# Two turned tiles instead of eight, v in runs for four, half-array third blocks, single row sums: a linear-attention and token-mixer kernel on one Trainium2 core

## The chip, the cores and the metric

The kernel runs on one core of a Trainium2 chip. The core has a matrix engine (TensorE, PE in the profile; its weight loads are PEld), a vector engine (VectorE, DVE), a scalar engine (ScalarE, ACT), a general engine (GpSimd, POOL) and a queue engine (SyncE, SP) that here only issues transfers. Each engine works through its own list of instructions in order. Sixteen DMA engines carry the transfers that SP and POOL issue. SBUF is the on-chip memory, PSUM the eight accumulator banks of PE. The metric is the device time of one execution in microseconds (us); lower is better.

## What is computed

Inputs `r, k, v, w, a, b` have the shape 4 x 8 x 768 x 40 (batch, heads, time, width), in 32-bit floats. A recurrence over time gives 768 rows of 320 numbers (8 heads x 40) for each of the four batches, and a mixer with one matrix over tokens and two over channels follows:

```python
for t in range(S):
    y[:, :, t] = np.einsum('bhd,bhde->bhe', rt, state)
    Sa = np.einsum('bhde,bhe->bhd', state, at)
    state_decay = state * wt[:, :, None, :] - np.einsum('bhd,bhe->bhde', Sa, bt)
    state = state_decay + np.einsum('bhd,bhe->bhde', vt, kt)
...
theta = x @ w_theta                       # x: the y of all heads side by side
zr, zi = x * np.cos(theta), x * np.sin(theta)
yr = np.einsum('ts,bsd->btd', w_tok_r, zr)
yi = np.einsum('ts,bsd->btd', w_tok_i, zi)
u = x + yr + yi
return u + np.maximum(u @ w_ch, 0.0)
```

## The kernel before

**Tiles.** Time is cut into tiles of 128 steps: six for each batch, 24 in all, numbered 0 to 23. A tile passes through these steps; the names are those of the program's list.

- *Loads.* w of every tile comes by one load of 160 KB (`raw_w`, line 465), 1,024 pieces of 160 bytes. r comes for two tiles at once in "runs": eight steps in a row are one piece of 1,280 bytes, 320 KB in all (line 481). For tiles below `RUNS` (8), v comes in runs too, and for tiles below `TURNED` (8) also k, b and a. All other k, b, a and v come by single loads of 160 KB (line 465). Buffers: four for w and for k and b, six for a and v. SP issues all loads in list order and stands still where a buffer has not been read yet.
- *Decay.* ACT takes the logarithm of w (`ln`, line 509); PE sums it over the tile (`cs`, line 518); ACT exponentiates (`exp`, or `exp1` and `ew` from tile 8 on).
- *Features of an unturned tile.* POOL multiplies k and b (`kb`) and a (`ah`) by the decays (line 493) and casts v (line 499). PE turns 16 blocks, or twelve where v came in runs (`tt`, line 419), and ACT or DVE evicts them to `feat` (`et`, lines 452 and 456).
- *Features of a turned tile.* Casts put the runs of k, b and a of two tiles into the order for turning (line 499), PE turns them into PSUM (`tkbr`, `tar`), PE also forms the summed logarithms in turned form (`csT`, line 604), ACT exponentiates them (lines 611 and 613), and DVE multiplies the turned k, b and a out of PSUM (lines 625 and 628). k and b are then turned back (`tbk`). v in runs is cast, turned (`to`), evicted by ACT (line 642) and turned back (`tb`, line 653).
- *Scores.* Products of k and a, b and a, v and r, nu and r in eight matmuls on array halves each (line 668): `spsi`, `sphi`, `slv`, `slu`. DVE multiplies by a triangular mask while it evicts (line 676), or ACT evicts (line 678) and POOL clears the triangle (line 680).
- *Recurrence and output.* Small products (lines 707 to 745) give the correction nu and the new state; lines 821 to 834 give the tile's output x.

**The mixer.** For two tiles at a time, x is turned in blocks of 128 columns (`xt`). The 320 columns of a tile are two blocks and a half; the buffers `xp` and `up` have 64 further columns of zeros behind the two tiles, so that each tile's third block can be read 128 wide, and the third block of the weights `wth` and `wch` has zeros in its lower 64 rows. `mixed` (line 804) runs six matmuls of 320 columns for a pair, three for each tile. ACT takes sine and cosine (line 859), and POOL forms z (line 493). After a batch, `mix_row` (line 881) multiplies z by the token matrices: twelve matmuls of 320 columns for each tile, the two tiles of a pair into the two banks of one double bank, then one DVE addition for both (`uadd2`, line 891). u is turned (`ut`), `mixed` multiplies by `wch`, DVE adds (line 915), and SP stores (line 918). Tiles 22 and 23 go through the mixer one by one.

**Order.** Nothing is ordered by the chip. `Plan.add` numbers some 1,370 operations; `ORDER` is a written-out list of these numbers, and each engine gets its operations in that order. `HOMES` gives the PSUM banks in the order in which they are taken. `PICK` names the operations that run in their other form: another engine, or a turn of whole blocks (line 424) instead of array halves (line 419). `WARM` puts fill matmuls (line 983) in front of some operations. Row and column weights are loaded by POOL (lines 927 and 935).

**Modes.** An operation on PE uses the whole array or its two halves of 64 rows, two matmuls at a time; the list mixes both.

Of the kernel before, what the change touches and what calls it, by code (L numbers as in the profile page):

```python
# [10 lines left out]
BF16 = mybir.dt.bfloat16  # L11
# [7 lines left out]
RUNS = 8  # L19
TURNED = 8  # L20
LATE = 8
ORDER = [
# [225 lines left out]
def kernel(  # L248
# [14 lines left out]
    nc = tc.nc  # L263
# [26 lines left out]
    def load(i):  # L290
# [5 lines left out]
        if i < TURNED:  # L296
            return ([("raw_w", s), raw_w[s], src(w)],)
# [98 lines left out]
    for t in (wth, wch):  # L396
        nc.vector.memset(t[rows(1), 2], 0.0)
# [64 lines left out]
    def loads(i):  # L462
# [8 lines left out]
        if i < RUNS:  # L471
            sets.append((v, raw_o[i // 2 % 3], "o"))
# [559 lines left out]
```

## Time and profile before

| | us |
|---|---|
| three runs | 201.14, 203.02, 204.42 |
| median | 203.02 |
| profiled execution, its span (the page gives no other time of it) | 201.1 |

| | instructions | busy us |
|---|---|---|
| PE | 4,254 | 185.6 |
| DVE | 270 | 165.1 |
| ACT | 298 | 161.6 |
| POOL | 166 | 138.1 |

A row of the page's groups has the line, the engine, the operation, its output and inputs with their shapes, how often, then the busy time in us, the mean duration in ns, and the idle time of the engine just before with what ended it. A row of a timeline has the start, the time taken, the engine, the line and what was done. PE's matmuls overlap: a duration contains the way through the array, so what one matmul costs PE is read from start to start. A row of the windows table has a stretch of the span, the busy time of each engine in it, the clock that PE was granted, the busy share of the DMA engines and what they moved. Consecutive instructions on ACT and DVE overlap by about a tenth of a microsecond.

### The profile page before, as it was taken

The numbers are of one execution on the slowest core, as the hardware profiler recorded it, in microseconds if no ns is written. First come the engines' busy times: TensorE is split into PE (matmuls) and PEld (weight loads), VectorE is DVE, ScalarE is ACT, GpSimd is POOL, SyncE is SP. The second block draws the span as 40 slices with busy tenths as digits, with TensorE's granted clock in tenths as the row PEclk, the third lists the DMA queues.
The fourth block names the chain that finished last, engine by engine and source line by source line (L and its number), as shares of the span: only waits on it lengthen the run. The fifth ranks groups of instructions, "written<-read, shape, count | busy, mean of one in ns | idle before, by whom it ended". The sixth has DMA issues, their size and how long they took to land.

```text
span 201.1 us, 9549 instructions
## 1 busy us (share of the span) xinstructions
PE 185.6 (92%) x4254; PEld 148.0 (74%) x4254; DVE 165.1 (82%) x270; ACT 161.6 (80%) x298; POOL 138.1 (69%) x166
## 2 busy tenths in 40 slices
PE   7689898996799898999999999999999999999992
PEld 7467686875787776787786878877887877877761
DVE  7599899997899899898988898798796859872462
ACT  2699999987899899878999979798999859585000
POOL 6355346790498989889959973979988984659000
PEclk9999999999999999999999999999999999999999
DMA  5999978999839999989999799736894010000332
GB/s 150 268 324 312 255 186 182 241 167 201 143 56 196 184 162 191 175 180 176 193 162 205 161 169 262 138 68 133 152 211 139 0 68 3 3 3 0 134 113 83
DMA packets 104888, 30.90 MB, mean 154 GB/s; under 512 B 92432, under 2 KB 104848, under 8 KB 104848
## 3 DMA queue, kind: packets, MB, share of 16 engines
q1 hardware_dynamic: 102416, 27.53, 62.2%
q0 software_dynamic: 2432, 2.77, 8.2%
q8 instruction: 33, 0.54, 1.1%
q14 instruction: 7, 0.06, 0.1%
HBM read 29.13 MB, written 3.93 MB: 164 GB/s over the span
## 4 chain that ended last, share of the span: by engine, by line
PE 61%; ACT 17%; DVE 14%; issue 2%; DMA 2%; SPq 1%; ACTq 0%
PE ps L881 19%; PE ps L668 8%; PE ps L804 8%; PE ps L419 8%; PE ps L424 4%; DVE lam L676 3%; PE ps L827 3%; DVE psi L676 3%; DMA raw_w<-in_w_dram 2%; ACT feat L452 2%; PE ps L712 2%; PE ps L745 2%; PE ps L724 2%; ACT exw L613 2%; PE ps L707 2%
## 5 line engine op out<-in xcount | busy, mean ns | idle before, releaser
L676 DVE TENSOR_TENSOR lam<-ps,mask_p 128x1024 bf16<-128x1024 f32 x37 | 44.9, 1219 | 4.9 <-PE ps L668 4.7
L881 PE MATMUL ps<-z,wtok 128*128 128x320 bf16 x288 | 47.5, 299 | 0.0
L493 POOL TENSOR_TENSOR z<-cs,xp 128x640 bf16<-128x640 f32 x21 | 29.8, 1430 | 2.8 <-ACT cs L859 2.8
L881 PEld LDWEIGHTS <-wtok 128*128 128x128 bf16 x288 | 24.9, 97 | 9.0
L493 POOL TENSOR_TENSOR kb<-raw_kb,ex 128x640 bf16<-128x640 f32 x16 | 22.9, 1431 | 4.3 <-DMA raw_kb<-in_b_dram 2.1
L668 PEld LDWEIGHTS <-feat 64*128 64x128 bf16 x576 | 18.3, 94 | 7.9 <-issue 5.3
L676 DVE TENSOR_TENSOR psi<-ps,mask_p 128x1024 bf16<-128x1024 f32 x18 | 21.8, 1216 | 0.3 <-PE ps L668 0.2
L676 DVE TENSOR_TENSOR phi<-ps,mask_n 128x1024 bf16<-128x1024 f32 x16 | 19.5, 1220 | 2.2 <-PE ps L668 2.1
L668 PE MATMUL ps<-feat 64*128 64x128 bf16 x384 | 18.6, 217 | 2.3 <-DVE phi L676 0.7
L827 PE MATMUL ps<-kb,lam 128*128 128x40 bf16 x384 | 15.6, 180 | 0.8 <-issue 0.8
L680 POOL TENSOR_SCALAR_AFFINE_SELECT lam<-lam 128x1024 bf16<-128x1024 bf16 x11 | 12.0, 1093 | 4.3 <-ACT lam L678 4.3
L827 PEld LDWEIGHTS <-lam 128*128 128x128 bf16 x384 | 13.8, 96 | 1.2 <-issue 0.9
L452 ACT COPY feat<-ps 128x1024 f32<-128x1024 f32 x14 | 14.2, 1020 | 0.7 <-PE ps L419 0.6
L728 ACT ACTIVATE nu<-ps 128x320 bf16<-128x320 f32 x24 | 10.8, 450 | 4.7 <-PE ps L724 4.5
L680 POOL TENSOR_SCALAR_AFFINE_SELECT phi<-phi 128x1024 bf16<-128x1024 bf16 x8 | 8.8, 1100 | 8.3 <-ACT phi L678 8.3
L642 ACT COPY rT<-ps 128x512 bf16<-128x512 bf16 x24 | 13.5, 602 | 1.2 <-PE ps L419 1.2
L493 POOL TENSOR_TENSOR ah<-raw_a,ex 128x320 bf16<-128x320 f32 x16 | 12.9, 807 | 2.2 <-ACT ex L540 2.1
L452 ACT COPY uT<-ps 128x384 f32<-128x384 f32 (+1 forms) x10 | 4.6, 463 | 11.8 <-PE ps L424 5.9
L915 DVE SCALAR_TENSOR_TENSOR oo<-ps,up 128x640 f32<-128x640 f32 x11 | 9.0, 822 | 6.0 <-PE ps L804 6.0
L509 ACT ACTIVATE lw<-raw_w 128x320 bf16<-128x320 f32 x24 | 11.7, 493 | 2.2 <-DMA raw_w<-in_w_dram 1.2
L625 DVE TENSOR_TENSOR feat<-ps,exi 128x512 bf16<-128x512 bf16 x16 | 10.4, 683 | 2.7 <-ACT exi L611 2.3
L718 ACT CAST nx<-ps 128x320 bf16<-128x320 f32 x24 | 10.5, 438 | 2.4 <-PE ps L712 2.1
(156 smaller groups left out, 557.1 us busy)
## 6 DMA issues: line engine op xcount, KB each, us to landing
raw_w<-in_w_dram SPq DMA_DIRECT2D x24, 160.0 KB, 4.6
raw_r<-in_r_dram SPq DMA_DIRECT2D x12, 320.0 KB, 4.8
out_dram<-oo SPq DMA_DIRECT2D x11, 320.0 KB, 3.1
raw_v<-in_v_dram SPq DMA_DIRECT2D x16, 160.0 KB, 4.6
raw_kb<-in_k_dram SPq DMA_DIRECT2D x16, 160.0 KB, 4.3
raw_kb<-in_b_dram SPq DMA_DIRECT2D x16, 160.0 KB, 4.4
raw_a<-in_a_dram SPq DMA_DIRECT2D x16, 160.0 KB, 4.4
raw_kb<-in_b_dram SPq DMA_DIRECT2D x4, 320.0 KB, 4.9
```

The costliest lines, as they stand in the source:

```text
L419: nc.tensor.transpose(out=dst[:, c, n * 64:n * 64 + 64], in_=block[rows(c)], identity=ident[rows(c), rows(c)])
L452: nc.scalar.copy(out=to, in_=source)
L493: pool = ("POOL", lambda: nc.gpsimd.tensor_tensor(out=dst, in0=in0, in1=in1, op=ALU.mult))
L509: add("ACT", "ln", i, lambda: nc.scalar.activation(out=heads(lw)[:, :, 0:D], in_=raw_w[s4], func=AF.Ln), 473, [("raw_w", s4)], [("lw", s2) ...
L642: add("ACT", "e" + nm, i + x, lambda x=x, dst=dst: nc.scalar.copy(out=dst.rearrange("p g (t q) -> p g t q", q=8), in_=ps(pr).bitcast(BF16) ...
L668: nc.tensor.matmul(t[:, q, g, :], lhsT=lhs[rows(q), g, :], rhs=rhs[rows(q), g, :], start=True, stop=True)
L676: add("DVE", kindm, i, lambda: nc.vector.tensor_tensor(out=flat, in0=whole(), in1=mask.to_broadcast([128, 2 * G, 128]), op=ALU.mult), 1217 ...
L680: add(None, "sel", i, None, 0, dkeys, dkeys, alts=(("POOL", lambda: nc.gpsimd.affine_select(out=flat, in_=flat, pattern=[[0, 2 * G], [1, 1 ...
L728: add("ACT", "enu", i, lambda: nc.scalar.mul(out=nu[:, :, 0:D], in_=ps(pk)[:, 0:DM].rearrange("p (h d) -> p h d", h=H), mul=-1.0), 437, [p ...
L804: nc.tensor.matmul(out, lhsT=lhs[:, 3 * c + kt, :], rhs=wt[:, kt, :], start=kt == 0, stop=kt == 2)
L827: nc.tensor.matmul(t[:, h * D:h * D + D], lhsT=lam[:, n, p, g, :], rhs=kb[:, n, h, 0:D], start=first and n == 0, stop=n == 1, skip_group_c ...
L881: nc.tensor.matmul(to, lhsT=wtok[t % NCH][:, c, s, :], rhs=z[:, c, s], start=s == 0 and c == 0, stop=s == NT - 1 and c == 1)
```

## The change

Six things change.

- `TURNED` goes from "below 8" to tiles 0 and 1, `RUNS` from "below 8" to tiles 0 to 3. Tiles 2 to 7 load k, b and a singly and form them on POOL; tiles 4 to 7 load v singly too.
- The zero columns of `xp` and `up` go. The 640 columns of two tiles are turned as five blocks; the middle one holds the last 64 columns of the first tile and the first 64 of the second. For the second tile `wth` and `wch` hold the rows a second time, shifted by 64, so there are four loads for each instead of two.
- For a pair `mixed` becomes two operations: four matmuls over whole blocks, and two over half blocks, one on each array half, into the two banks.
- A row sum takes one bank, and each tile has its own addition (`uadd`).
- `ORDER`, `HOMES` and `PICK` are new as a whole. Among other things the loads of w for tiles 1 and 0 now stand first in SP's list.
- `WARM` has two entries (44 fill matmuls) instead of nine.

The diff without the lists, whose old and new lines are left out:

```diff
-RUNS = 8
-TURNED = 8
+RUNS = frozenset(range(4))
+TURNED = frozenset(range(2))
...
-WARM = {19: (38, 0), 20: (2, 3), 21: (3, 2), 30: (6, 3), 44: (2, 3), 58: (4, 3), 106: (1, 2), 264: (2, 4), 274: (1, 4)}
+WARM = {21: (38, 0), 20: (6, 1)}
...
-        if i < TURNED:
+        if i in TURNED:
             return ([("raw_w", s), raw_w[s], src(w)],)
...
-                () if i < RUNS else ([("raw_v", i % 6), raw_v[i % 6], src(v)],))
+                () if i in RUNS else ([("raw_v", i % 6), raw_v[i % 6], src(v)],))
...
-    xp_t = padded("xp", [128, 2 * DM + 64], NX // 2, lambda t: t[:, 2 * DM:])
-    up_t = padded("up", [128, 2 * DM + 64], 2, lambda t: t[:, 2 * DM:])
-    xT_t = sb("xT", [128, 6, 128], BF16, NXT)
-    uT_t = sb("uT", [128, 6, 128], BF16, 2)
+    xp_t = sb("xp", [128, 2 * DM], BF16, NX // 2)
+    up_t = sb("up", [128, 2 * DM], BF16, 2)
+    xT_t = sb("xT", [128, 5, 128], BF16, NXT)
+    uT_t = sb("uT", [128, 5, 128], BF16, 2)
...
-    wth = consts.tile([128, 3, DM], BF16, name="wth")
-    wch = consts.tile([128, 3, DM], BF16, name="wch")
-    for t in (wth, wch):
-        nc.vector.memset(t[rows(1), 2], 0.0)
+    wth = consts.tile([128, 5, DM], BF16, name="wth")
+    wch = consts.tile([128, 5, DM], BF16, name="wch")
...
     def blocks_of(t):
-        return [t[:, c * DM + m:c * DM + m + 128] for c in range(t.shape[1] // DM)
-                for m in (0, 128, 256)]
+        return [t[:, m:m + 128] for m in range(0, t.shape[1], 128)]
...
+        def whole():
+            for c in range(2):
+                for kt in range(2):
+                    nc.tensor.matmul(ps(pk)[:, c, 0:DM], lhsT=lhs[:, 3 * c + kt, :],
+                                     rhs=wt[:, 3 * c + kt, :], start=kt == 0, stop=False,
+                                     skip_group_check=True)
+
+        def third():
+            for c in range(2):
+                nc.tensor.matmul(ps(pk)[:, c, 0:DM], lhsT=lhs[rows(c), 2, :],
+                                 rhs=wt[rows(c), 2, :], start=False, stop=True,
+                                 skip_group_check=True)
+        add("PE", kind, q, whole, 4 * mm(320), [lkey] + wkeys, [pk], at=at, new=(pk, 2),
+            tail=tail(320))
+        add("PE", kind + "3", q, third, mm(320), [lkey] + wkeys, [pk], at=at, mode=64,
+            tail=tail(320))
...
         for t in group:
+            pk = ("ps", "row", t)
             for s in range(NT):
-                def chunk(t=t, s=s):
-                    to = ps(pk)[:, 0:DM] if alone(q) else ps(pk)[:, t - q, 0:DM]
+                def chunk(t=t, s=s, pk=pk):
                     for c in range(2):
-                        nc.tensor.matmul(to, lhsT=wtok[t % NCH][:, c, s, :], rhs=z[:, c, s],
-                                         start=s == 0 and c == 0, stop=s == NT - 1 and c == 1)
+                        nc.tensor.matmul(ps(pk)[:, 0:DM], lhsT=wtok[t % NCH][:, c, s, :],
+                                         rhs=z[:, c, s], start=s == 0 and c == 0,
+                                         stop=s == NT - 1 and c == 1)
...
+            add("DVE", "uadd", t, lambda t=t, pk=pk: nc.vector.tensor_tensor(
+                out=u_of(t), in0=ps(pk)[:, 0:DM], in1=x_of(t), op=ALU.add), 488,
+                [pk, x_key(t)], [u_key(t)], at="row")
...
             pieces = ((dst[:, 0:2, :], src[0:256, :].rearrange("(a p) d -> p a d", p=128)),
-                      (dst[rows(0), 2, :], src[256:320, :]))
+                      (dst[rows(0), 2, :], src[256:320, :]),
+                      (dst[:, 3:5, :], src[64:320, :].rearrange("(a p) d -> p a d", p=128)),
+                      (dst[rows(1), 2, :], src[0:64, :]))
```

More of the change, by code (lines that the diff above doesn't have):

```diff
@@ L547, in prep @@
         fast = i < 2
-        if i >= TURNED:
+        if i not in TURNED:
             product("kb", i, kb[:, :, :, 0:D], raw_kb[s4],
@@ L798, in mixed, with go @@
         pk = ("ps", kind, q)
-        def go():
-            for c in range(1 if alone(q) else 2):
-                out = ps(pk)[:, 0:DM] if alone(q) else ps(pk)[:, c, 0:DM]
+        if alone(q):
+            def go():
                 for kt in range(3):
-                    nc.tensor.matmul(out, lhsT=lhs[:, 3 * c + kt, :], rhs=wt[:, kt, :],
+                    nc.tensor.matmul(ps(pk)[:, 0:DM], lhsT=lhs[:, kt, :], rhs=wt[:, kt, :],
                                      start=kt == 0, stop=kt == 2)
-        add("PE", kind, q, go, (3 if alone(q) else 6) * mm(320), [lkey] + wkeys, [pk], at=at,
-            new=(pk, 1 if alone(q) else 2), tail=tail(320))
+            add("PE", kind, q, go, 3 * mm(320), [lkey] + wkeys, [pk], at=at, new=(pk, 1),
+                tail=tail(320))
+            return
+        def whole():
[12 more added lines that the diff above has]
+        add("PE", kind + "3", q, third, mm(320), [lkey] + wkeys, [pk], at=at, mode=64,
+            tail=tail(320))
     def readout(i):
@@ L851, in sines @@
         cs, pk = cs_t[n % NCS], ("ps", "th", q)
-        mixed("th", q, xT_t[n % NXT], wth, [("wth", c) for c in range(2)], ("xT", n % NXT))
+        mixed("th", q, xT_t[n % NXT], wth, [("wth", c) for c in range(4)], ("xT", n % NXT))
         wide_ = 1 if alone(q) else 2
@@ L904, in channels @@
                uT_t[n][:, 0:len(blocks)], [("uT", n)], at="row")
-        mixed("ch", q, uT_t[n], wch, [("wch", c) for c in range(2)], ("uT", n), at="row")
+        mixed("ch", q, uT_t[n], wch, [("wch", c) for c in range(4)], ("uT", n), at="row")
         ck, oo = ("ps", "ch", q), oo_t[n]
@@ L928, in mixer_weights @@
                     out=to, in_=part), 580, [], [(key, c)], at="rel",
-                    work=260 if c else 1030)
+                    work=260 if c % 2 else 1030)
     def wtok_block(tb):
```

31 lines of the change are left out of this document (10 added, 21 removed), and 199 rows, old and new, of tables (HOMES, ORDER, PICK).

## The prediction

> **What bounds the kernel now.** I read the page first (busy shares, slices, queues), then the table by windows, then the chain of waits in order of time, and last the timelines of single engines around the places where the limit changes.
>
> ```profile
> PE 185.6 (92%) x4254; PEld 148.0 (74%) x4254; DVE 165.1 (82%) x270; ACT 161.6 (80%) x298; POOL 138.1 (69%) x166
> ...
> DMA  5999978999839999989999799736894010000332
> ...
> q1 hardware_dynamic: 102416, 27.53, 62.2%
> q0 software_dynamic: 2432, 2.77, 8.2%
> ```
>
> No engine is alone at the limit, and the DMA row is at 9 for most of the first 26 slices (5.03 us each). The windows separate the stages:
>
> ```profile
> core 0: us, PE busy (x) PEld busy (x) DVE busy (x) ACT busy (x) POOL busy (x), PEclk, DMA share, GB/s
> 0.00:80.60 80.60, 69.71 (x1798) 57.72 (x1799) 72.77 (x147) 71.27 (x135) 52.33 (x76) 1.00 0.92 201
> 10.00:20.00 10.00, 8.77 (x225) 7.14 (x223) 9.76 (x13) 9.93 (x22) 5.42 (x8) 1.00 1.09 318
> 50.00:60.00 10.00, 8.60 (x254) 7.46 (x249) 9.07 (x13) 9.31 (x18) 6.95 (x9) 1.00 0.57 101
> 80.00:85.00 5.00, 5.00 (x90) 3.70 (x89) 4.03 (x6) 4.50 (x10) 4.64 (x5) 1.00 0.98 171
> 87.70:201.10 113.40, 108.81 (x2294) 84.74 (x2288) 86.32 (x117) 84.05 (x152) 80.01 (x84) 1.00 0.55 118
> ...
> 190.00:201.00 11.00, 6.96 (x66) 4.59 (x63) 5.36 (x9) 0.80 (x2) 0.00 (x0) 0.97 0.29 100
> ```
>
> Up to 80.6 us DVE (72.77) and ACT (71.27) are nearly full and PE has 1,798 of its 4,254 matmuls behind it. From 87.7 us PE is busy for 108.81 of 113.40 us and the others have 27 us or more to spare. The chain shows the handover from DVE to PE:
>
> ```profile
> 75.39 1.13 DVE psi L676
> 76.53 1.79 DVE z L492
> 78.31 1.15 DVE phi L676
> 79.50 0.40 PE ps L668 x8
> 79.90 0.38 PE ps L881 x2
> ```
>
> So there is a first stage of about 80 us that DVE and ACT set, and a second that PE sets. The third resource, transfers, is hidden in the first stage, but not by much. Tile 12 marks the handover, and its last load and first product are these:
>
> ```profile
> 74.09 1.19 SPq L465 DMA_DIRECT2D raw_kb<-in_k_dram  x1
> ...
> 82.01 1.43 POOL L493 TENSOR_TENSOR kb<-raw_kb,ex 128x640 bf16<-128x640 f32 x1
> ...
> raw_kb<-in_k_dram SPq DMA_DIRECT2D x16, 160.0 KB, 4.3
> ```
>
> With the median of 4.3 us to landing, the load issued at 74.09 is there at 78.4; the product starts at 82.01. Only 3.6 us lie between, so the first stage can shrink by little before the transfers set it.
>
> **Fewer turned tiles: the engines.** Tiles 2 to 7 (six tiles) lose the decays in turned form and the products from PSUM:
>
> ```profile
> L625 DVE TENSOR_TENSOR feat<-ps,exi 128x512 bf16<-128x512 bf16 x16 | 10.4, 683 | 2.7 <-ACT exi L611 2.3 <-PE ps L419 0.5
> L613 ACT ACTIVATE exw<-ps,sign_col 128x512 f32<-128x512 f32 x8 | 5.6, 704 | 0.0
> L611 ACT ACTIVATE exi<-ps 128x512 f32<-128x512 f32 x8 | 4.9, 613 | 0.5 <-PE ps L604 0.5
> L493 POOL TENSOR_TENSOR kb<-raw_kb,ex 128x640 bf16<-128x640 f32 x16 | 22.9, 1431 | 4.3 <-DMA raw_kb<-in_b_dram 2.1 <-PE ps L827 1.1 <-DMA raw_kb<-in_k_dram 0.7
> L493 POOL TENSOR_TENSOR ah<-raw_a,ex 128x320 bf16<-128x320 f32 x16 | 12.9, 807 | 2.2 <-ACT ex L540 2.1
> L452 ACT COPY feat<-ps 128x1024 f32<-128x1024 f32 x14 | 14.2, 1020 | 0.7 <-PE ps L419 0.6
> ...
> L983 PE MATMUL ps<-busy 128*128 128x128 bf16 x59 | 6.7, 280 | 1.1 <-DVE busy L314 1.1
> ```
>
> DVE loses 18 products of 0.68 (12.3 us) and three evictions of that size, and by the list takes over three large evictions and five small ones: some 8 us less. ACT loses 6 x (0.70 + 0.61) = 7.9 us and eleven small evictions, and gains three large ones (1.02) and six casts: some 10 us less. POOL gains 6 x (1.43 + 0.81) = 13.4 us of products, loses twelve casts of 0.72 (8.6 us; a row further down shows one) and gains four DMA issues of about 0.6: some 7 us more, 59 of 80.6, so it does not become the limit. PE loses more turns here than it gains, in a stage in which it waits anyway. If nothing else bound the first stage, DVE's 8 us would come off it.
>
> **Fewer turned tiles: the transfers.** The edit turns k, b and a of six tiles and v of four (22 loads of 160 KB in 160-byte pieces) out of 11 loads of 320 KB in 1,280-byte pieces. A 160 KB load: between 80 and 85 us hardly anything else runs, 171 GB/s at share 0.98, so 163.84 KB takes 0.96 x 0.98 = 0.94 us of all 16 engines. A 320 KB load: q1 has 62.2% of 201.1 = 125.1 us; 88 small loads take 82.7, and the 40 units of 320 KB (28 loads, and stores worth 12) the other 42.4, so 1.06 each. POOL's queue: 8.2% is 16.5 us for 2,704 KB (12 rows of weights at 192, two pieces at 160, two at 40), so 1.17, 0.98 and 0.24.
>
> Ahead of tile 12's last load stand, by the old list, 38 small loads, 22 large ones, eight weight rows and one piece of each size: 35.7 + 23.3 + 9.4 + 1.2 = 69.6 us. By the new list it is 58, 12, nine rows and four pieces of each size: 54.5 + 12.7 + 10.5 + 4.9 = 82.6 us. That is 13.0 us more, and more than the first stage holds.
>
> ```profile
> 0.80 0.72 SPq L481 DMA_DIRECT2D raw_kb<-in_b_dram  x1
> ...
> 2.24 0.60 SPq L465 DMA_DIRECT2D raw_w<-in_w_dram  x1
> ...
> 4.44 0.72 POOL L499 CAST z<-raw_kb 128x640 bf16<-128x640 f32 x1 [0.88 <-DMA raw_kb<-in_b_dram]
> ...
> SPq L481 <- POOL r L499: 4.6, 1, 4.6
> ```
>
> The first load (1.06 of work) has landed at 4.44, so a landing comes 3.4 us after the work ahead of it. The old landing at 78.4 is then 69.6 + 3.4 + 5.4 of idle queue: the 0.57 in 50:60 is most of that, and the last row shows why, SP held until a buffer was read. In the new order readers run ahead of the queue (DVE and ACT have 8 us less to do), so I take 1 us of idle, between 0 and the old 5.4. Tile 12's last load, raw_a, lands at 82.6 + 3.4 + 1.0 = 87.0. Then come its product (0.81), the turn on PE, the eviction (1.02), and the scores.
>
> ```profile
> 85.78 0.41 PE L419 MATMUL ps<-ident,kb 64*128 64x64 bf16 x16
> 86.02 0.28 PE L419 MATMUL ps<-ident,ah 64*128 64x64 bf16 x8
> ...
> 87.47 0.40 PE L668 MATMUL ps<-rT,feat 64*128 64x128 bf16 x8
> 87.70 0.39 PE L668 MATMUL ps<-feat 64*128 64x128 bf16 x8
> ...
> 97.52 0.98 PE L804 MATMUL ps<-wth,xT 128*128 128x320 bf16 x6
> 98.43 0.40 PE L668 MATMUL ps<-feat 64*128 64x128 bf16 x8
> ...
> 185.12 0.98 PE L804 MATMUL ps<-wch,uT 128*128 128x320 bf16 x6
> 185.94 4.24 PE L881 MATMUL ps<-z,wtok 128*128 128x320 bf16 x30
> 190.01 0.50 PE L424 MATMUL ps<-ident,up 128*128 128x128 bf16 x6
> 190.35 0.98 PE L881 MATMUL ps<-z,wtok 128*128 128x320 bf16 x6
> ```
>
> Eight blocks turn in 86.02 - 85.78 = 0.24, so sixteen in 0.48. With 0.3 for handovers the scores of tile 12 start at 89.6; before, it was 87.70 (fourth row).
>
> **The mixer products.** Six 320-column matmuls take 185.94 - 185.12 = 0.82, 0.136 each. Eight half-array matmuls of 128 columns take 87.70 - 87.47 = 0.23, two at a time in 0.058; for 320 columns 0.14 a pair. So a pair of tiles goes from 0.82 to 4 x 0.136 + 0.14 = 0.68. Eighteen of the 22 come after tile 12's scores: 2.5 us less. Turning five blocks in place of six (0.057 a whole block by 190.35 - 190.01, 0.03 in halves) goes there from 6 whole and 12 halved calls, 4.2 us, to 4 and 14, 3.2. Changes of mode: the six matmuls before a half-array operation took 98.43 - 97.52 = 0.91, 0.09 more; after tile 12's scores the new list has 85 changes, the old 73: 1.1 us more. Small differences of the list give 0.4. PE's work after that point is 2.8 us less.
> The Trainium skill, "TensorEngine Tiling (Array Packing)", Key Properties, says that changing the tiling mode drains TensorE. If a drain meant the whole tail of a matmul (0.98 against 0.82, 0.16) it would be 1.9 us for those twelve and the sum 0.8 higher; the rows above say 0.09.
>
> **The rest.** Single row sums cost DVE about 22 x 0.49 - 11 x 0.82 = 1.8 us, under 27 us of idle time; if that cover were gone, 1.8. What banks and order can give back after 87.7 is bounded by PE's idle time there, 4.6 us, most of it the tail of the last store; a loss is bounded by nothing that this trace shows and is kept in the range. Twenty of the 59 fills go (59 take 6.7 us): 2.3 us of PE at most, in the stage in which it waits, so nothing; the clearings that go lie ahead of DVE's first data, nothing either. The loads of w are issued first instead of at 2.24: ACT starts some 1.4 us sooner, in a stage that transfers set, so nothing again, and 1.4 less if that were not so.
>
> **Sum.** 89.6 + 113.4 - 2.8 = 200.2 us against the profiled 201.1. Of the profiled execution only this span is given; the median of the runs, 203.02, lies 1.9 above it: 202. With idle queue from 0 to 5.4 us it is 201.1 to 206.5; and since in 10:20, with large loads in it, 1.09 of work went into the time of one, the 28 us of large loads and weights may cost 2.5 less: 198.6.
>
> **Rivals.** *The transfers stay hidden* (23%): readers and loads overlap better than my sum, DVE and ACT still set the first stage, 8 us go there and 2.8 on PE: 190.3, with the 1.9, 192. For it: DVE and ACT are at 90% of the first stage. Against it: only 3.6 us in hand against 13.0 us of new work.
> *The load queue is held* (27%), on the slower side: SP issues in list order, and the new list puts loads for tiles 15 to 18 ahead of tile 14's; each waits for its buffer with the nearer loads behind it. With the old idle of 5.4 and one more wait of the longest kind shown (4.6), 10 us instead of 1: 209.2, with the 1.9, 211. It decides once idle passes 6 us (207). For it: 5.4 us happened before, with less to move. Against it: the readers have less to do.
> *The halves run one after the other* (5%), so that the change does not do what it says: 18 x 0.136 = 2.4 more, 204.6. Against it: the pairs at 87.47.
> *The clock falls* (3%). PE would wait some 27 us in the first stage, in longer gaps than now. Only the last window has a clock under 1.00 (0.97), and there PE has stopped. A fall to half for some 3 us lost in a gap costs 1.5 us of PE work, if it comes just ahead of the handover: 203.7. The Trainium skill, "TensorE: Matmul & The Clock Gate", Part 1, puts the clock at half after an idle window of about 3.4 us; by that a wait of such length would cost 1.7. PE has no such gap in this trace before its end.
>
> **How the numbers follow.** The forecast, transfers take over the first stage and little changes, has 42%; its time, 202, is the prediction, its own range 199 to 207. A measurement of this kernel tells about 2% from no change: 199.0 to 207.1. Faster: 23% of the first rival and 3 of the forecast's lower end, 26%. Slower: 27% and 3 of its upper end, 30%. Within: 44%. The range reaches to both rivals' times, 191 to 211.
>
> **What would show it.** Right: the first slices' DMA row at 9 without gaps to 85 us or more, POOL's products and ACT's ln waiting for DMA in tiles 4 to 12, DVE and ACT visibly below 90% there, tile 12's scores near 89 us, mixer calls of 0.68. Wrong: tile 12's scores near 80 us (first rival), or after 95 us with SP's queue waiting for buffers for 10 us (second); pairs of third blocks at 0.27; a PEclk below 1 in a slice before 90 us.

## The result, and the profile after

| | before | after |
|---|---|---|
| median of four runs, us | 202.08 | 209.09 |
| lowest to highest, us | 200.97 to 204.42 | 207.28 to 209.78 |
| profiled execution: span, us | 201.1 | 207.3 |
| start of tile 12's scores, us | 87.7 | 93.9 |
| from there to the end of the span, us | 113.4 | 113.4 |

The changed kernel is slower: its time is 1.034 of the time before, with a 95% interval of 1.025 to 1.043. The forecast was 202. The profiled execution after took 208.99 us, 1.7 more than its span. Ratios, here and below, leave out executions more than 1.5% above the fastest of their kernel, while medians hold all of them; the profiled executions of o_short11, o_third and n_fill73 are such slow ones.

The page of the changed kernel, in the lines that answer to those shown of before:

```profile
PE 183.1 (88%) x4094; PEld 142.2 (69%) x4094; DVE 158.4 (76%) x256; ACT 154.7 (75%) x279; POOL 144.7 (70%) x169
...
PEclk9975967999995998799999999999999999999999
DMA  6999989998999989999999999895991101002122
...
q1 hardware_dynamic: 122304, 27.53, 65.6%
q0 software_dynamic: 3136, 3.18, 10.1%
```

DVE has 6.7 us less to do, ACT 6.9 less, POOL 6.6 more, PE 2.5 less by its busy time; that part came near the forecast, but for ACT, which was to lose some 10. A slice is 5.18 us. The DMA row stands at 8 or 9 from the second slice to the twenty-seventh (140 us), where before it had slices of 3 and 7, and but for one slice at 5 up to 155 us. PEclk was at 9 everywhere in the profile before; now it falls below at four places ahead of 90 us.

The windows of the changed kernel (stretch, its length, busy time of PE, weight loads, DVE, ACT and POOL, clock, DMA share, GB/s):

```profile
0.00:80.60 80.60, 63.74 (x1555) 51.97 (x1555) 59.59 (x112) 59.95 (x108) 55.20 (x81) 0.87 1.00 184
10.00:20.00 10.00, 8.34 (x184) 6.20 (x184) 8.88 (x11) 8.21 (x16) 9.33 (x13) 0.67 1.15 216
20.00:30.00 10.00, 6.62 (x193) 5.41 (x187) 6.43 (x9) 5.85 (x12) 5.52 (x8) 0.84 1.02 172
60.00:70.00 10.00, 8.16 (x195) 6.83 (x196) 6.33 (x10) 9.11 (x14) 9.45 (x12) 0.66 1.06 192
93.90:207.30 113.40, 106.07 (x2265) 79.84 (x2257) 88.54 (x130) 83.59 (x152) 76.57 (x77) 1.00 0.58 124
```

In the first 80.6 us the DMA share is 1.00 instead of 0.92, and DVE is busy for 59.59 us instead of 72.77: DVE and ACT no longer set this stage. Two things could: the transfers, which are full, or PE, whose clock was at half for 24 us ahead of tile 12's scores (the mean clock of the whole span is 0.942). These are waits of the changed kernel up to tile 12's scores (who waits, for whom, us in all, how often, longest), the largest first:

```profile
DVE lam L673 <- PE ps L665: 8.1, 4, 3.2
ACT lw L506 <- DMA raw_w<-in_w_dram: 6.1, 4, 2.8
...
POOL kb L490 <- DMA raw_kb<-in_b_dram: 4.5, 1, 4.5
...
POOL v L496 <- DMA raw_v<-in_v_dram: 3.5, 3, 2.1
...
POOL kb L490 <- DMA raw_kb<-in_k_dram: 3.2, 3, 2.7
```

The largest wait is one of DVE for PE, which by itself would fit either reading. All waits of POOL and ACT for DMA sum to 25.3 us here; before, up to 87.7 us, they summed to 15.2.

Behind tile 12 there are such waits too. A timeline of the changed kernel, first POOL, then PE:

```profile
129.82 0.45 POOL L496 CAST v<-raw_v 128x320 bf16<-128x320 f32 x1
133.11 1.43 POOL L490 TENSOR_TENSOR kb<-raw_kb,ex 128x640 bf16<-128x640 f32 x1 [2.84 <-DMA raw_kb<-in_k_dram]
134.49 1.10 POOL L677 TENSOR_SCALAR_AFFINE_SELECT lam<-lam 128x1024 bf16<-128x1024 bf16 x1
...
134.25 0.18 PE L839 MATMUL ps<-kb,lam 128*128 128x40 bf16 x1
135.64 0.24 PE L839 MATMUL ps<-kb,lam 128*128 128x40 bf16 x3 [1.21 <-POOL lam L677]
```

POOL stands 2.84 us for k of a later tile. Queued behind that product on POOL is the clearing of `lam`, which the output of tile 15 needs, and PE stands 1.21 us for it. So PE, which the prediction had running almost without a wait from tile 12 on, still depends on loads there: it is busy for 106.07 of 113.40 us, where it was busy for 108.81 before.

### The profile page after: what moved, and what is told of

It reads as the page before. It is cut to its first block, busy times and chain, and to the rows that moved or that the text cites. A ratio compares the mean times of both kernels' runs of the same rounds, so it can differ in the third digit from the quotient of the medians.

```text
span 207.3 us, 9200 instructions
## 1 busy us (share of the span) xinstructions
PE 183.1 (88%) x4094; PEld 142.2 (69%) x4094; DVE 158.4 (76%) x256; ACT 154.7 (75%) x279; POOL 144.7 (70%) x169
## 5 line engine op out<-in xcount | busy, mean ns | idle before, releaser
L673 DVE TENSOR_TENSOR lam<-ps,mask_p 128x1024 bf16<-128x1024 f32 x38 | 46.2, 1219 | 11.0 <-PE ps L665 10.5
L490 POOL TENSOR_TENSOR kb<-raw_kb,ex 128x640 bf16<-128x640 f32 x22 | 31.4, 1427 | 21.8 <-DMA raw_kb<-in_k_dram 6.4
L449 ACT COPY feat<-ps 128x1024 f32<-128x1024 f32 (+1 forms) x17 | 16.9, 1001 | 6.4 <-PE ps L416 6.0
L490 POOL TENSOR_TENSOR ah<-raw_a,ex 128x320 bf16<-128x320 f32 x22 | 17.8, 811 | 3.6 <-DMA raw_a<-in_a_dram 1.6
L898 DVE TENSOR_TENSOR up<-ps,xp 128x320 bf16<-128x320 f32 x22 | 10.7, 488 | 6.2 <-PE ps L893 5.9
L709 PE MATMUL ps<-v,psi 128*128 128x40 bf16 x192 | 11.3, 185 | 2.8 <-POOL psi L677 2.8
L416 PE MATMUL ps<-ident,kb 64*128 64x64 bf16 x352 | 9.5, 197 | 4.6 <-POOL kb L490 4.4
L846 DVE TENSOR_TENSOR xp<-ps,ex 128x320 bf16<-128x320 f32 x22 | 10.6, 486 | 3.1 <-PE ps L839 3.0
L677 POOL TENSOR_SCALAR_AFFINE_SELECT lam<-lam 128x1024 bf16<-128x1024 bf16 x10 | 11.0, 1097 | 2.6 <-ACT lam L675 2.6
L833 PE MATMUL ps<-gd,rT 128*128 128x80 bf16 x80 | 12.8, 202 | 0.0
```

What stands on the lines that cost most here:

```text
L416: nc.tensor.transpose(out=dst[:, c, n * 64:n * 64 + 64], in_=block[rows(c)], identity=ident[rows(c), rows(c)])
L449: nc.scalar.copy(out=to, in_=source)
L490: pool = ("POOL", lambda: nc.gpsimd.tensor_tensor(out=dst, in0=in0, in1=in1, op=ALU.mult))
L673: add("DVE", kindm, i, lambda: nc.vector.tensor_tensor(out=flat, in0=whole(), in1=mask.to_broadcast([128, 2 * G, 128]), op=ALU.mult), 1217 ...
L677: add(None, "sel", i, None, 0, dkeys, dkeys, alts=(("POOL", lambda: nc.gpsimd.affine_select(out=flat, in_=flat, pattern=[[0, 2 * G], [1, 1 ...
L709: nc.tensor.matmul(t[:, h * D:h * D + D], lhsT=psi[:, p, g, :], rhs=vb[:, h, 0:D], start=first and h == 0, stop=True, skip_group_check=True)
```

## The experiments

Fifteen kernels were run beside the kernel before. Names with o_ start from the kernel before, names with n_ from the changed one. "Scores" is the start of tile 12's scores in the profiled execution, "rest" the time from there to the end of the span. Ratios are to the kernel before, run on the same chip, with their 95% interval; for n_fill none was formed.

| kernel | median us | ratio | scores | rest |
|---|---|---|---|---|
| n_long22 | 198.59 | 0.984 [0.975, 0.994] | 86.4 | 112.1 |
| n_longall | 196.19 | 0.969 [0.959, 0.979] | 83.7 | 109.1 |
| o_longall | 206.98 | 1.028 [1.016, 1.039] | 92.7 | 112.8 |
| o_short11 | 212.89 | 1.052 [1.042, 1.062] | 98.2 | 115.3 |
| n_fill | 210.58 | none | 93.5 | 110.1 |
| n_need | 205.65 | 1.016 [1.005, 1.027] | 88.5 | 114.3 |
| o_third | 203.29 | 0.995 [0.989, 1.002] | 90.4 | 113.1 |
| o_nofill | 203.67 | 1.006 [1.001, 1.011] | 87.0 | 114.9 |
| n_latelong | 205.65 | 1.015 [1.009, 1.021] | 93.7 | 109.2 |
| o_latelong | 203.53 | 1.003 [0.998, 1.007] | 86.7 | 113.2 |
| n_need2 | 207.51 | 1.026 [1.021, 1.031] | 95.5 | 110.4 |
| n_need2_wch | 209.41 | 1.034 [1.030, 1.037] | 97.2 | 110.5 |
| n_fill73 | 209.49 | 1.027 [1.015, 1.039] | 92.6 | 115.3 |
| n_need3 | 207.31 | 1.025 [1.018, 1.031] | 90.6 | 114.8 |
| n_need3_fill73 | 210.46 | 1.040 [1.032, 1.048] | 93.0 | 114.6 |

**The size of the pieces, in both kernels.** The transfers theory says that the small pieces of the newly single loads cost the time. In these kernels (n_long22, n_longall, o_longall, o_short11, n_latelong, o_latelong) the loads named bring the same number of bytes in other pieces; the data then arrive in another order of steps, or from another batch, so the output is not the reference's. Nothing else differs.

```diff
 def src(ap):
+    if ap is not w and 2 <= i < 8:        # n_long22; n_longall and o_longall: all single loads
+        return ap[bi, :, ci * C:(ci + 1) * C, :].rearrange("h (t q) d -> t h (q d)", q=8)
     return ap[bi, :, ci * C:(ci + 1) * C, :].rearrange("h t d -> t h d")
...
+    if nm in "kba" and 2 <= i < 8 or nm == "o" and 4 <= i < 8:        # o_short11
+        raw = raw.rearrange("p c (h d) -> p (c h) d", d=D)
+        runs = ap[bi:bi + 2, :, ci * C:(ci + 1) * C, :].rearrange("b h t d -> t (b h) d")
```

> New kernel, but the 22 loads that the change moved to 160-byte pieces (k, b, a of tiles 2 to 7, v of tiles 4 to 7) read as many bytes in 1,280-byte pieces from other places of the same tensors, so the numbers are not the reference's. Transfers theory: 22 x 0.41 = 9 us of transfer go from ahead of tile 12, its scores start near 87 instead of 93.9 and the time is 7 to 9 us under the new kernel's 209, 200 to 202. Clock theory (half clock in four stretches is what costs): transfers alone change little, 205 to 209. List theory (the new order of the engines' work is worse by itself): 207 to 209.

> New kernel with all 110 small loads in 1,280-byte pieces from other places, so the numbers are not the reference's; 45 us of transfer go. Transfers theory: transfers are no limit any more, DVE and ACT set the first stage with 8 to 10 us less work than before the change, and the time is 190 to 194. Clock theory: the clock stays up only if PE's waits go too; 195 to 200. List theory: 205 or more.

> Kernel before with all its 88 small loads in 1,280-byte pieces from other places, so the numbers are not the reference's; 36 us of transfer go. If transfers were hidden before the change, as the prediction says: 199 to 203, no change. If they already set a part of its first stage: under 198.

> Kernel before with the eleven loads in runs of tiles 2 to 7 (k, b, a of three pairs, v of two) read in 160-byte pieces from other places, so the numbers are not the reference's; its list stays. 11 x 0.82 = 9 us of transfer come ahead of tile 12. Transfers theory: 3.6 us of them were in hand, the rest shows: 204 to 208. Clock theory and list theory: no change, 200 to 203.

Two of the four are mirror images. n_long22 is the changed kernel with the old number of packets; o_short11 is the old kernel with the new number:

| median, us | about 102,500 packets | about 122,200 packets |
|---|---|---|
| the old operations and lists | 202.08 | 212.89 (o_short11) |
| the new operations and lists | 198.59 (n_long22) | 209.09 |

Down each column the new operations and lists take 3.5 to 3.8 us off; along each row the small pieces add 10.5 to 10.8. The medians come from separate measurements, but the ratios to the kernel before say the same: 1.034 / 0.984 = 1.050 for the pieces in the new kernel, 1.052 in the old, each good to about 1%. So within 1% or so the two effects add, and the small pieces are the cause of the loss. Their price includes whatever the clock does in answer to them, which the next part looks at. How the gain of 3.5 us divides among the parts of the change (turned tiles, mixer, lists) is not separated. The waits of POOL and ACT for DMA up to tile 12's scores go the same way: 6.7 us in n_long22, 25.3 in the changed kernel, 38.8 in o_short11.

All four forecasts of the time were missed. n_long22 is faster than the 200 to 202 of the transfers theory. o_short11 is 4.9 us over the end of its 204 to 208, which had 3.6 us of cover in it: there was none. n_longall, at 196.19, lies above the 190 to 194 of the transfers theory and inside the 195 to 200 of the clock theory, so with the transfers out of the way something else is left; its tile 12 starts at 83.7, 4.0 us earlier than before, where DVE's 8 us were to come off. Next, from the page of n_long22, packets and busy share of its load queue, and then its windows:

```profile
q1 hardware_dynamic: 102592, 27.53, 64.0%
...
0.00:86.40 86.40, 71.79 (x1837) 58.47 (x1839) 72.62 (x127) 70.18 (x129) 67.19 (x93) 0.96 1.00 205
86.40:198.50 112.10, 105.56 (x2265) 79.74 (x2257) 88.26 (x130) 83.26 (x152) 76.63 (x77) 0.99 0.56 121
```

The queue was busy for 0.640 x 198.5 = 127.0 us instead of 0.656 x 207.3 = 136.0: 9.0 us for 22 loads, 0.41 each, about the 0.94 - 1.06 / 2 = 0.41 of the prediction's own prices. Here 9.0 us of transfer work are worth 10.5 us of time. The Trainium skill, "DMA: Bandwidth & Descriptors", Specifications, asks for transfers of at least 512 bytes for the full rate; these runs agree, 160 KB at 0.94 us against 0.53.

o_longall missed in the other direction: cheaper loads made the old kernel slower. Its windows and a row of its waits:

```profile
20.00:25.00 5.00, 2.34 (x57) 1.86 (x54) 2.74 (x5) 2.29 (x7) 0.72 (x1) 0.76 0.97 252
25.00:30.00 5.00, 5.00 (x83) 4.33 (x83) 3.54 (x4) 3.72 (x9) 2.99 (x4) 0.55 0.09 23
...
POOL psi L682 <- DMA raw_kb<-in_b_dram: 5.8, 1, 5.8
```

A load of b came late, 5.8 us of waiting, and then the queue stood almost empty (0.09). The suspects were the first loads of w, which had become cheap as well and changed who is served when. Two further runs split the loads by tile:

```diff
+    if i >= 13:        # n_latelong; o_latelong: if i >= 8
+        return ap[bi, :, ci * C:(ci + 1) * C, :].rearrange("h (t q) d -> t h (q d)", q=8)
```

> The kernel before with the single loads of tiles 8 to 23 alone (80 of its 88) in pieces of 1,280 bytes; the loads of w of tiles 0 to 7, which the earlier run with all 88 had as well, stay as they are. That run lost 3.6 us by tile 2. If that loss came from the w loads, which overtook the loads of r, k, b and a in the first 25 us: 198 to 203 us here, tile 2's scores at 24 to 25. If cheaper loads do harm wherever they are: 205 to 208.

> The changed kernel with the single loads of tiles 13 to 23 alone (55 of its 110) read in pieces of 1,280 bytes instead of 160, so that the same bytes come in another order of steps and their output differs; the loads ahead of tile 12 are as before. If transfers hold the second stage too (POOL's product for tile 18 stood 2.84 us waiting for k, and PE behind it): tile 12's scores within 2 us of 93.9, but the rest shorter, 106 to 107.5 us from there to PE's end instead of 109.9, and 203 to 206 us. If the second stage's waits come from ACT's and POOL's order alone: 109 to 110.5 from there and 207 to 210.

With the early w loads left alone the old kernel keeps its time (203.53), although 80 of its 88 single loads are cheap. So the loss of o_longall lies in the start, in the w loads of tiles 0 to 7 (that they overtook the others is inferred, not seen), and the loads of tiles 8 to 23 are hidden in the old kernel. n_latelong did what the transfers theory says: tile 12's scores at 93.7 as in the changed kernel, and the rest 4.2 us shorter. Its windows, and POOL at the place where the changed kernel stood 2.84 us:

```profile
0.00:93.70 93.70, 74.61 (x1835) 60.02 (x1837) 69.42 (x127) 70.50 (x128) 67.98 (x93) 0.93 0.99 191
93.70:202.90 109.20, 105.13 (x2267) 79.65 (x2259) 88.15 (x130) 83.17 (x152) 76.83 (x77) 0.99 0.42 123
...
129.35 1.43 POOL L492 TENSOR_TENSOR kb<-raw_kb,ex 128x640 bf16<-128x640 f32 x1 [0.27 <-PE ps L841]
```

The wait for k is gone in this execution. By the medians the late single loads cost 3.4 us (205.65 against 209.09; the ratios, 1.015 [1.009, 1.021] and 1.034 [1.025, 1.043], lie apart), and that at a mean clock that is no higher (0.933 to 0.966). In which stage they cost it is less sure: the profiled execution of n_fill, below, has the loads of the changed kernel and yet a rest of 110.1.

**The clock.** The rival theory: PE's waits let the clock fall, and slow PE work costs the time. n_fill keeps PE active inside its waits.

```diff
-WARM = {21: (38, 0), 20: (6, 1)}
+WARM = {21: (38, 0), 20: (6, 1), 19: (20, 6), 41: (6, 2), 30: (5, 0), 73: (15, 2),
...
+        458: (41, 0), 426: (9, 6), 200: (6, 4), 550: (6, 4), 527: (40, 2)}
```

> The changed kernel with 307 more of its fill matmuls (21 places, each in PE's queue ahead of an operation for which PE waited more than 0.3 us in the first 92 us, as many as fit into that wait; each writes only its first product's bank, ahead of the operation that overwrites it). Nothing else is changed; the loads and their order are the same. If the lost clock is what cost the time (24 us at half before tile 12's scores): no stretch at half, or one, tile 12's scores at 88 to 91 us instead of 93.9, 202 to 206 us. If the transfers alone set the first stage and the fall of the clock only filled waits: tile 12's scores stay at 93 to 95 and the time at 207 to 210.

The page of n_fill (its clock), then its windows, and last POOL at the product that stood 2.84 us for k in the changed kernel:

```profile
PEclk9999999999999999999999999999999999999997
...
0.00:93.50 93.50, 86.88 (x2142) 73.60 (x2144) 70.76 (x127) 71.06 (x128) 67.27 (x93) 1.00 1.02 188
93.50:203.60 110.10, 105.64 (x2267) 79.84 (x2261) 88.31 (x130) 83.31 (x152) 76.78 (x77) 0.99 0.58 125
...
130.01 1.43 POOL L490 TENSOR_TENSOR kb<-raw_kb,ex 128x640 bf16<-128x640 f32 x1 [0.80 <-PE ps L893]
```

The clock did not fall before the end, and tile 12's scores came at 93.5 instead of 93.9. This profiled execution was the fastest of four (205.28, the others 209.17 to 212.24). But PE was busy for 86.88 of 93.50 us, some 16 of them with the added fills, so the fills may have eaten what the clock gave. A smaller dose tells the two apart, and the kernel before without its own small fills asks the same from the other side:

```diff
+WARM = {21: (38, 0), 20: (6, 1), 41: (3, 2), 73: (6, 2), 108: (5, 2), 166: (16, 6),      # n_fill73
+        146: (5, 5), 208: (8, 4), 458: (14, 0), 527: (16, 2)}
...
-WARM = {19: (38, 0), 20: (2, 3), 21: (3, 2), 30: (6, 3), 44: (2, 3), 58: (4, 3), 106: (1, 2), 264: (2, 4), 274: (1, 4)}
+WARM = {19: (38, 0), 20: (2, 3), 21: (3, 2)}      # o_nofill
```

> The changed kernel with 73 more fill matmuls (3.9 us of PE at full clock; eight places, each inside a wait that PE had there and at most 0.9 us long, in or before the windows after which the clock fell). The earlier 307 fills kept the clock at 1.00 but took 18 us of PE themselves, so that run can't tell a lost clock from lost transfers. If the half clock (24 us of it before tile 12's scores) cost time on the path: mean clock 0.98 or more, tile 12's scores at 89.5 to 91.5, 203 to 206 us. If PE only had longer waits in place of slow work, because the transfers set the pace: scores at 93 to 94.5 with the same clock, 207 to 210.

> The kernel before without the 16 fill matmuls (six places between the second and the seventh tile) that the changed list doesn't have; the 43 fills at the start stay. They compute nothing that is read. If the fills hold the clock of before: a stretch at half in the first 30 us and 204 to 208 us. If they don't matter: 201 to 203 us and no stretch at half before the end.

With 73 fills the mean clock of the four runs was 0.967 to 0.988, against 0.942 to 0.966 in the changed kernel, and the median 209.49 against 209.09. The scores, at 92.6, lie between what the two theories said. The ratio, 1.027 [1.015, 1.039], rests on two runs (206.44 and 209.39), and fills take PE time themselves: on top of n_need3, further down, the same 73 cost 3.1 us. So this pair leaves room for a gain of some 4 us by the clock.

Two comparisons on record need no fills. Among the changed kernel's own runs one took 208.99 us at a mean clock of 0.942 and one 209.19 at 0.966, with 10 us less at half. And at the same mean clock, 0.965 and 0.966, n_long22 took 197.31 and the changed kernel 209.19. So the fallen clock is not what carries the loss. The likely reason, argued and not shown, is that PE works slowly where it would otherwise wait: even at half clock it was busy for only 63.74 of the first 80.6 us.

Half clock is not free everywhere. Without its 16 small fills the old kernel's clock did fall (half for 6.8 us at 8.4), and its time rose by 0.6% [0.1, 1.1], 1.1 us, between its two forecasts. (The kernel before is not free of falls either: over its 46 runs beside the others the mean clock goes from 0.977 to 1.000.) What the half clock adds to the changed kernel's time is open, up to a few microseconds.

**The order of the loads.** SP's new list has loads for tiles 13, 15, 16, 18 and 21 ahead of nearer ones. Four runs keep the operations of all other engines in their order and move SP's loads (and in one the four issues of the channel weights on POOL). An extract of SP's order, tile by tile:

```
changed:  ... k11, b13, v11, v13, a13, r10/11, v12, r12/13, w12, k12, b12, a12, w13, b15, w14, ...
n_need2:  ... k11, b11, a11, v11, r10/11, w12, k12, b12, a12, v12, w13, w14, k13, b13, ...
```

> The changed kernel with the same operations and the same order on PE, DVE, ACT and POOL, but SP's loads in the order in which their first users stand in the list (no load is put ahead of the last reader of its buffer). The transfer work issued ahead of tile 12's last load falls by 3.8 us, that ahead of tile 14's by 4.7 and of tile 16's by 6.6. If transfers set the first stage: tile 12's scores at about 90, 203 to 206 us, and less wait for DMA on PE's side engines. If only the clock counts: no change beyond what a shifted window does, 206 to 210.

> The changed kernel with SP's loads in the order of the times at which PE needed their data in the run with all loads in long pieces (the loads for tile 13, r for 12, 15, 16, 18 and 21 no longer stand ahead of those for tiles 12, 14 and 16). Work ahead of tile 12's last load is 4.8 us less, ahead of tile 14's 6.6, of tile 15's 7.7, of tile 18's 8.7. If transfers set both stages: tile 12's scores at 88 to 89.5, no wait of POOL for k of tile 18, 106.5 to 108.5 us from there to PE's end, 200 to 203 us. If their order doesn't matter because all of them are late: as the earlier re-sorting, 205 to 207.

> The same, and the four pieces of the channel weights (2.9 us of transfer work, first read after tile 12's scores) issued by POOL after the product kb of tile 12 instead of in the first 10 us. If transfers set the first stage: tile 12's scores 2 to 3 us earlier than without that, 85.5 to 87.5, and 198 to 201 us. If POOL's four issues at that place cost more than the transfers gain: no earlier than without, or a wait of the mixer for the weights at about 95 us.

> The changed kernel with the loads for tiles up to 12 in the order of the first re-sorting (scores at 88.5 there) and those for tiles 13 to 23 in the order of need (106.9 us from tile 12's scores to PE's end there). The two together: 88 to 90, then 106.5 to 108, span 198 to 201, 199.5 to 203 us. If the two stages trade against each other, since the transfer work is the same in all orders: 204 to 207.

> The same with the 73 fills. If the half clock cost time: 2 to 3 us less than without the fills, 197 to 201 us, which would be under both kernels. If it cost none: as without the fills, or up to 2 us more, since the waits lie elsewhere in this order and the fills then delay PE.

Only n_need gained clearly, 3.4 us by the medians and as the transfers theory had it. n_need2 missed its 200 to 203 and came just over the 205 to 207 of its second theory; the later weights of n_need2_wch brought no earlier scores (97.2). Where the scores come early (88.5, 90.6) the rest is long (114.3, 114.8), and where the rest is short (110.4, 110.5) the scores are late (95.5, 97.2). It looks as if the stages trade against each other, but these are single executions, and the clock differs too. The clock of n_need, then of n_need2:

```profile
PEclk9976997599999999999999998899999999999999
...
PEclk9965899969996999979999999999999999999999
```

n_need has a stretch at half behind tile 12 (from 125.1 us), where PE sets the time; so have n_need3, n_fill73 and n_need3_fill73, all with a rest over 114, while n_need2 has none there and n_need2_wch only the last 2.4 us of one. Whether their long rests come from the loads or from the clock is open.

n_need2 also shows that tile 12's own load does not decide. Its rows, SP's issue of that load and POOL's products of tile 12:

```profile
76.97 2.50 SPq L383 DMA_DIRECT2D raw_a<-in_a_dram  x1
...
90.18 1.43 POOL L411 TENSOR_TENSOR kb<-raw_kb,ex 128x640 bf16<-128x640 f32 x1 [0.72 <-ACT ex L451]
92.17 0.81 POOL L411 TENSOR_TENSOR ah<-raw_a,ex 128x320 bf16<-128x320 f32 x1 [0.57 <-ACT ex L458]
```

The same of the changed kernel, with a row of its issue list for the time around 85 us (3.9 us from issue to landing):

```profile
85.11 1.32 SPq L462 DMA_DIRECT2D raw_a<-in_a_dram  x1
...
raw_a<-in_a_dram SPq DMA_DIRECT2D x1, 160.0 KB, 3.9
...
89.00 1.43 POOL L490 TENSOR_TENSOR kb<-raw_kb,ex 128x640 bf16<-128x640 f32 x1 [0.25 <-ACT ex L530]
90.53 0.81 POOL L490 TENSOR_TENSOR ah<-raw_a,ex 128x320 bf16<-128x320 f32 x1
```

In the changed kernel the load lands at 89.0 and is read at 90.53, with no wait for it. In n_need2 it is issued 8 us earlier and read 1.6 us later. There POOL has stood for loads of other tiles up to then, 11.5 us for `raw_a` alone, which fits with POOL, ACT and PE being late. n_need3, the two orders together, came to 207.31, just over what a trade between the stages was to give, and with fills it came out 3.1 us worse than without; no reordered version is faster than the kernel before.

**The mixer alone.**

```diff
-            for c in range(1 if alone(q) else 2):
...
+            for c in range(2):
+                for kt in range(2):
+                    nc.tensor.matmul(ps(pk)[:, c, 0:DM], lhsT=lhs[:, 3 * c + kt, :],
+                                     rhs=wt[:, 3 * c + kt, :], start=kt == 0, stop=False,
+                                     skip_group_check=True)
+            for c in range(2):
+                nc.tensor.matmul(ps(pk)[:, c, 0:DM], lhsT=lhs[rows(c), 2, :],
+                                 rhs=wt[rows(c), 2, :], start=False, stop=True,
+                                 skip_group_check=True)
```

> The kernel before, with one part of the change alone: the third blocks of the mixer's pairs on the two array halves, five blocks of 128 columns turned instead of six, the weights' third piece loaded to both halves. Order, banks, loads and engines are those of before. The prediction's price is 0.14 us less on each of 22 paired calls and half a block less in each turn: 198.5 to 200.5 us. If third blocks on halves run one after the other: within 1 us of before. If shorter PE work opens a window that lets the clock fall: over 203, with a stretch at half.

Its ratio is 0.995 [0.989, 1.002]: 0.9 us of the 2.5 to 4.5 expected, and not clear of noise. That is as little as serial halves were to give, and the third forecast came in part: the clock was at half for 6.8 us in the profiled execution, whose scores come at 90.4. The run also carries the four further weight loads of the change, 2.4 us of transfers by the prediction's prices. So its time does not price the mixer; its timeline does. A timeline of PE in o_third, one call with its successor, and then one in the changed kernel:

```profile
103.93 0.70 PE L805 MATMUL ps<-wch,uT 128*128 128x320 bf16 x4
104.57 0.31 PE L809 MATMUL ps<-wch,uT 64*128 64x320 bf16 x2
104.81 0.72 PE L805 MATMUL ps<-wch,uT 128*128 128x320 bf16 x4
```

```profile
102.14 0.71 PE L807 MATMUL ps<-wth,xT 128*128 128x320 bf16 x4
102.78 0.31 PE L813 MATMUL ps<-wth,xT 64*128 64x320 bf16 x2
102.93 0.31 PE L416 MATMUL ps<-ident,up 64*128 64x64 bf16 x10
```

From start to start the four whole matmuls take 0.64, not 4 x 0.136 = 0.54: the change of mode to the halves is in it. The pair takes 0.15, so the halves do run side by side; where whole blocks follow it is 0.24, with the change back. A call costs 0.79 or 0.88, against 0.91 and 0.82 before (the prediction's rows at 97.52 and 185.12).

## Why the prediction was wrong

**The mechanism was right.** Transfers did take over the first stage; DVE and ACT fell as forecast and were no longer its limit; POOL and ACT wait for DMA for 25.3 us up to tile 12's scores, where it was 15.2. The price of a single load was right too (0.41 us more per 160 KB, 0.41 measured). Two terms of "89.6 + 113.4 - 2.8" were not: the first came out 4.3 too low, the last did not appear in the time, and 7.1 is the whole distance from 200.2 to the span of 207.3.

**"With 0.3 for handovers the scores of tile 12 start at 89.6": 93.9.** The step that failed is to let one load, tile 12's last, stand for the whole stage. Only 2.0 of the 4.3 us are that load's. It landed at 89.0 instead of 87.0: the packet times in the trace up to 86.6 us already sum to 86.1 us of work, with some 57 of the 58 small loads done, not 82.6. The pieces of the mixer's weights cost 1.0 more than priced, the rows 0.6, and small packets of other kinds, never counted, 2.0. The other 2.3 us come after the landing. The load's product starts 1.6 us later, behind another product on POOL, and from its start to the scores it takes 3.4 us, where the forecast had 2.6, because ACT and PE do other work first. n_need2 shows the same more strongly: there the load is early and the scores are later still. Up to 93.9 us the DMA share is 0.99 and there is no moment without a packet in flight, where the kernel before had 2.3 us of such moments up to 87.7. So the transfers had nothing in hand to make up a delay with, and it is likely that a late load of any tile passes its delay on through POOL, ACT and PE, which work in order. The sum to make was that of all added transfer work against all idle time, not the landing of one load. One row was also misread: SP's 4.6 us for r, given as the reason for the idle queue at 50 to 60 us, lies behind 87.7; at that place SP stood 4.3 us for v.

**"PE's work after that point is 2.8 us less": the time after it is the same, 113.4.** PE's work did fall about as forecast: it is busy for 106.07 us there instead of 108.81. But it stands for 7.3 us instead of 4.6. What failed is that the term was taken off with no question what is late next. The transfers run, with one half-empty slice, to 155 us, 61 us past tile 12; cheaper loads there take 3.4 us off the time (n_latelong), and in its profile PE stands for 4.1 us. That it is waits for loads which give all of the 2.8 back is likely, but n_fill's one execution has few waits with the same loads, so it is not shown.

**"So a pair of tiles goes from 0.82 to ... 0.68": 0.79 or 0.88.** The forecast had the mode changes as a term of their own (1.1 us), so its sum was less wrong than the call's price. In the second stage all mixer calls together took 16.7 us from start to start, against 16.9 before, and the turns of x and u 5.5 against 6.0. The rest of what PE saved came from small operations that the new list turns in another form or puts beside others of their mode: the turns of the state and of nu, for instance, 4.3 instead of 5.3.

**The rivals.** *The transfers stay hidden* (23%, 192) would have needed 13 us of room; o_short11 shows that there was none, and with the old number of packets (n_long22) the kernel takes 198.6, not 192: its scores moved by only 1.3 us, with the DMA share still at 1.00. *The load queue is held* (27%, 211) came near in time but not in kind: SP's waits for buffers up to tile 12's scores fell, from 16.3 to 9.3 us, and the transfers ran on through them. *The halves run one after the other* (5%) is refuted by the 0.15. *The clock falls* (3%) happened, for 24 us instead of 3. By the runs at equal clock it does not carry the loss, and a few microseconds stay open; it was priced as work lost, while PE was busy for 63.74 of 80.6 us only. The argument against it, that PE had no long gap, held in the new trace as well (2.75 us at most) and did not keep the clock up.

## What to carry to other kernels

Where the DMA engines have no idle time left, count all the transfer work that a change adds, for every stage up to the last load, and take each microsecond of it as a microsecond of time (here 9.0 us became 10.5); cover that the old trace shows at one load is not cover for the rest. To separate transfers from engine work, change only the size of the pieces, in the old kernel and in the new one: the two differences then say whether the effects add. A fallen TensorE clock beside long waits need not be the cause: compare runs of equal clock before calling it one, since fills put into the waits change PE's work as well.

## What was not expected of the hardware

**The clock fell without a long gap.** Windows of the changed kernel just ahead of its four falls (PE's busy time is the third number), and then two windows after which it stayed up, one of the old kernel and one of the changed kernel:

```profile
10.10:13.50 3.40, 2.05 (x62) 1.43 (x61) 3.40 (x6) 3.04 (x5) 3.14 (x5) 1.00 1.08 218
23.70:27.10 3.40, 1.54 (x31) 1.06 (x30) 2.56 (x5) 2.09 (x4) 0.42 (x1) 1.00 1.07 189
57.80:61.20 3.40, 1.89 (x44) 1.48 (x43) 3.07 (x5) 0.97 (x2) 1.88 (x2) 1.00 0.99 174
78.30:81.70 3.40, 1.14 (x31) 0.96 (x28) 1.04 (x3) 1.75 (x4) 1.59 (x3) 1.00 0.83 163
```

```profile
50.10:53.50 3.40, 2.38 (x76) 1.97 (x72) 2.92 (x4) 3.40 (x9) 1.09 (x1) 1.00 0.66 117
...
150.00:153.40 3.40, 1.99 (x63) 1.51 (x60) 1.63 (x5) 1.92 (x5) 1.40 (x3) 1.00 1.09 248
```

PE is busy for 1.14 to 2.05 us of 3.40 ahead of the falls, and its longest gap up to tile 12 is 2.75 us; with 2.38 busy it did not fall, but nor did it with 1.99, so the busy time alone does not give the limit. The half clock then lasted 3.4 or 6.8 us. The Trainium skill, "TensorE: Matmul & The Clock Gate", Part 1, speaks of an idle window of about 3.4 us and of gaps longer than that; here the clock fell after a window in which PE was busy for 2.05 us, and the measurement decides.

**An issue can take long with no buffer to wait for.** Of two issues in a row in the changed kernel one takes 0.58 us and the next 3.20, and the timeline shows no wait of SP between them:

```profile
74.89 0.58 SPq L462 DMA_DIRECT2D raw_v<-in_v_dram  x1
75.52 3.20 SPq L462 DMA_DIRECT2D raw_a<-in_a_dram  x1
```

That SP is held because its queue is full is inferred. For it speaks the size of the pieces: the kernel before, whose single loads come in small pieces as well, has issues of up to 3.47 us, while with all loads in long pieces (n_longall) none takes over 1.9. So SP's issue times are no measure of when a load was wanted.
